# A spatial product of seven block products in place of eight, in a fused Fourier mixing and gated MLP kernel

## The chip, the cores and the metric

The kernel runs on one core of one Trainium2 chip. The metric is the device time of one execution in microseconds. Every kernel here was run several times, on a chip that also ran the kernel before; medians and ranges are given.

## The reference, cut to what matters

```python
X = np.fft.fft(np.fft.fft(x, axis=1), axis=2).real     # x: 8 batches, 3072 rows, 256 columns
h = np.maximum(X @ w_in, 0.0)                          # 1024 columns
u, v = h[..., :512], h[..., 512:]
v_n = (v - mean(v)) / np.sqrt(var(v) + 1e-06)          # row by row
v_s = np.einsum('ts,bsd->btd', w_spatial, v_n) + b_spatial[None, :, None]
out = (u * v_s) @ w_out
```

The heavy part is the spatial product: a 3072 x 3072 matrix times the 512 columns of v, for each of eight batches. The weights of that matrix are 0.01/3072 times a normal draw, and the bias beside it is 1. The output therefore hardly depends on the spatial product, and the comparison with the reference would not notice a mistake in it. For the experiments this means that a kernel with wrong block sums on purpose can still be called correct; where I did that, I say so.

Of the kernel before, what the change touches and what calls it, by code (L numbers as in the profile page):

```python
# [9 lines left out]
FP32 = mybir.dt.float32  # L10
# [23 lines left out]
NWR = 5  # L34
AHEAD = 4
# [13 lines left out]
VFIRST = [0, 1, 2, 4, 5, 7]  # L49
# [6 lines left out]
FOLD = [(2, 4), (8, 16), (18, 20)]  # L56
DCT = [36, 38, 40, 42]
VAT = [44 + (17 * i) // 4 for i in range(NPAIR)]
FOLD1 = [(12, 16), (24, 28), (36, 38)]
DCT1 = [40, 42, 44, 46]  # L60
VAT1 = [49 + (15 * i) // 4 for i in range(NPAIR)]
# [11 lines left out]
def kernel(  # L73
# [17 lines left out]
    wrpool = ctx.enter_context(tc.tile_pool(name="wrpool", bufs=NWR))  # L91
    wbpool = ctx.enter_context(tc.tile_pool(name="wbpool", bufs=3))
# [3 lines left out]
    upool = ctx.enter_context(tc.tile_pool(name="upool", bufs=8))  # L96
    gpool = ctx.enter_context(tc.tile_pool(name="gpool", bufs=6))
# [17 lines left out]
    bbc = const.tile([P, S], FP32)  # L115
# [19 lines left out]
    def load_x(b, a, xr):  # L135
        xt = xpool.tile([P, 8, D], FP32, name="xt", tag="xt")
        base = x.offset + b * S * D
        nc.sync.dma_start(out=xt[:, 0:4, :],
                          in_=bass.AP(x.tensor, base + (1 + a) * D,
                                      [[3 * D, P], [768 * D, 4], [1, D]]))  # L140
        nc.sync.dma_start(out=xt[:, 4:8, :],
                          in_=xr.rearrange("j p (r d) -> p j r d", r=3)[:, :, 2 - a, :])
        return xt[:, 0:4, :], view(xt, 7 * D, [[-D, 4], [1, D]])
# [13 lines left out]

    def load_w():
# [5 lines left out]
        wr = wrpool.tile([P, HW], FP32, name="wr", tag="wr")  # L164
# [14 lines left out]
    def cast_w(first=False):  # L179

        i = wstate["cast"]
        if i >= len(pieces):
            return
        c, g, r = pieces[i]
        wr = wrq[i]
        wbs[i] = wbpool.tile([P, HW], BF16, name="wb", tag="wb")
        src = wr if g % 2 == 0 else view(wr, HW - 1, [[-1, HW]])
        if first:
            nc.scalar.copy(out=wbs[i], in_=src)  # L189
        else:  # L190
            nc.gpsimd.tensor_copy(out=wbs[i], in_=src)  # L191
        wstate["cast"] = i + 1
        load_w()
# [23 lines left out]
    siota = bbc[:, 0:LQ]  # L217
# [11 lines left out]
    xs = xpool.tile([4 * B, D], FP32, name="xs", tag="xs")  # L229
# [48 lines left out]
    sp4 = spool.tile([4 * B, 6, 4 * B], FP32, name="sp4", tag="sp4", bufs=1)  # L278
# [77 lines left out]
    def fold_even(plus, rev):  # L356

        sm = fpool.tile([P, 4, D], FP32, name="sm", tag="sm")
        nc.vector.tensor_tensor(out=sm, in0=plus, in1=rev, op=ALU.add)
        e = ef  # L360
        nc.vector.tensor_copy(out=view(e, 0, [[129, 4], [128, 2]]),
                              in_=view(sm, 0, [[D, 4], [128, 2]]))
        nc.vector.tensor_tensor(out=e[:, :, 1:128], in0=sm[:, :, 1:128],
                                in1=view(sm, 255, [[D, 4], [-1, 127]]), op=ALU.add)
        evf = fpool.tile([P, 2, 129], FP32, name="evf", tag="evf")
        od = gxpool.tile([P, 2, 129], BF16, name="od", tag="od")
        ev = gxpool.tile([P, 2, 129], BF16, name="ev", tag="ev")
        nc.vector.tensor_tensor(out=od, in0=e[:, 0:2], in1=e[:, 2:4], op=ALU.subtract)
        nc.vector.tensor_tensor(out=evf, in0=e[:, 0:2], in1=e[:, 2:4], op=ALU.add)
        nc.vector.tensor_tensor(out=ev[:, 0], in0=evf[:, 0], in1=evf[:, 1], op=ALU.add)  # L370
        nc.vector.tensor_tensor(out=ev[:, 1], in0=evf[:, 0], in1=evf[:, 1],
                                op=ALU.subtract)
        return od, ev

    def fold_odd(plus, rev, od):


        df = plus
        nc.vector.tensor_tensor(out=df, in0=df, in1=rev, op=ALU.subtract)
        o = of  # L380
        nc.vector.tensor_tensor(out=o[:, :, 1:128], in0=df[:, :, 1:128],
                                in1=view(df, 255, [[df.ap[1][0], 4], [-1, 127]]),
                                op=ALU.subtract)
        ovf = fpool.tile([P, 2, P], FP32, name="ovf", tag="ovf")
        ho = gxpool.tile([P, 2, P], BF16, name="ho", tag="ho")
        he = gxpool.tile([P, 2, P], BF16, name="he", tag="he")
        nc.vector.tensor_tensor(out=ho, in0=view(o, 0, [[3 * P, 2], [1, P]]),
                                in1=view(o, 2 * P, [[-P, 2], [1, P]]), op=ALU.subtract)
        nc.vector.tensor_tensor(out=ovf, in0=o[:, 0:2], in1=o[:, 2:4], op=ALU.add)
        nc.vector.tensor_tensor(out=he[:, 0], in0=ovf[:, 0], in1=ovf[:, 1], op=ALU.add)  # L390
        nc.vector.tensor_tensor(out=he[:, 1], in0=ovf[:, 0], in1=ovf[:, 1], op=ALU.subtract)
        nc.vector.tensor_copy(out=view(ho, 0, [[P, 2], [1, 1]]),
                              in_=view(od, 129 + 128, [[-129, 2], [1, 1]]))
        return ho, he

    def specials():

        nb = 4 * B
        xe = gxpool.tile([nb, 129], BF16, name="xe", tag="xe", bufs=1)
        xo = gxpool.tile([nb, P], BF16, name="xo", tag="xo", bufs=1)  # L400
# [22 lines left out]
        sc = gxpool.tile([nb, 2, nb], BF16, name="sc", tag="sc", bufs=1)  # L423
# [17 lines left out]
    def specials_copy(pb):  # L441
        nc.vector.tensor_copy(out=spb, in_=pb[:, 0:2, :])
        nc.vector.tensor_copy(out=spb[0:1, 1, :], in_=pb[0:1, 2, :])

# [41 lines left out]
    def dct_odd(b, c, gx, eo):  # L486
# [17 lines left out]
        if b == 0 and c % 2 == 0:  # L504
            nc.scalar.activation(out=view(eo, EOW + c, [[4, n]]), in_=po_[:, 0:n],
                                 func=AF.Identity, bias=spb[:, 1, c:c + 1])
            return
        nc.vector.tensor_scalar(out=view(eo, EOW + c, [[4, n]]), in0=po_[:, 0:n],
                                scalar1=spb[:, 1, 4 * b + c:4 * b + c + 1],
                                scalar2=(sgn[:, 0:1] if c == 1 else None),  # L510
                                op0=ALU.add, **({"op1": ALU.mult} if c == 1 else {}))


    def v_rows(i, eo, pr, first):
# [3 lines left out]
        rs = spool.tile([P, 3], FP32, name="rs", tag="rs")  # L518
# [63 lines left out]
    def v_norm(i, v, pr):  # L582
        r, stt, mv, rs = pr.pop(i)
        k = 2 * GK * (i // GK) + i % GK
        nc.vector.reciprocal(out=rs[:, 0:2], in_=rs[:, 0:2])
        nc.vector.tensor_scalar(out=rs[:, 2:3], in0=mv[:, 0, 0:1], scalar1=rs[:, 0:1],  # L586
# [8 lines left out]
    def u_pair(c, dt, eo):  # L595
# [5 lines left out]
        for kt in range(2):  # L601
# [8 lines left out]
        nc.vector.tensor_tensor(out=view(um, TC - 1, [[-1, TC]]), in0=ps, in1=m_,  # L610
                                op=ALU.subtract)
        if c == 0:
            p1 = psM.tile([P, TC], FP32, name="pu1", tag="psM")
            for kt in range(2):
                nc.tensor.matmul(p1[:, 0:1], lhsT=weo[:, kt, wd],
                                 rhs=eo[:, kt, S // 2:S // 2 + 1], start=(kt == 0),
                                 stop=(kt == 1))
            nc.vector.tensor_copy(out=um[:, TC - 1:TC], in_=p1[:, 0:1])
# [8 lines left out]
    def gate(c, pw, ut):  # L627
        gt = gpool.tile([P, TC], BF16, name="gt", tag="gt")
        tm = tpool.tile([P, TC], FP32, name="tm", tag="tm")
        nc.vector.tensor_tensor(out=tm, in0=pw, in1=bbc[:, TC * c:TC * c + TC], op=ALU.add)  # L630
        nc.vector.scalar_tensor_tensor(out=gt, in0=ut, scalar=0.0, in1=tm, op0=ALU.max,  # L631
                                       op1=ALU.mult)
        return gt
# [32 lines left out]
    class Prep:  # L666
# [6 lines left out]
        def even(self, a):  # L673
            self.xt = xt0[a] if self.b == 0 else xin.pop((self.b, a))
            self.od, self.ev = fold_even(*self.xt)
            if self.b == 0:
                dct_part(a, (self.od, self.ev, None, None), self.pe0)

        def odd(self, a):
            ho, he = fold_odd(*self.xt, self.od)  # L680
            self.gx.append((self.od, self.ev, ho, he))
            if self.b > 0:
                if a + 1 < NA:
                    x_step(self.b, a + 1)
                else:
                    x_step(self.b + 1, 0)
# [9 lines left out]
        def v_steps(self, i):  # L696

            def va():
                if i == 0:
# [4 lines left out]
                    lambda: v_root(i, self.pr), lambda: v_norm(i, self.v, self.pr)]  # L704

        def v_first(self, i):
# [7 lines left out]
            if i > 0:  # L714
                v_norm(i - 1, self.v, self.pr)
# [3 lines left out]
        def steps(self):  # L719
# [3 lines left out]
            fold, dct, vat = (FOLD1, DCT1, VAT1) if self.b == 1 else (FOLD, DCT, VAT)  # L723
            if self.b == 1:
                st_[5].append(lambda: x_step(1, 0))
            for a in range(NA):
                s0, s1 = fold[a]
                st_[s0].append(lambda a=a: self.even(a))
                st_[s1].append(lambda a=a: self.odd(a))
# [3 lines left out]
            for i in range(NPAIR):  # L733
                for n, f in enumerate(self.v_steps(i)):
                    st_[vat[i] + n].append(f)
            return st_

    def load_wt(c, g):
# [140 lines left out]
```

## The kernel before: the parts that the change and the argument touch

Weights of the spatial product are turned and stored in HBM once, at the start. Later a batch streams them back as tiles of 768 KB (6 KB in a row for each of 128 partitions) into a ring of five buffers. Per batch there are six chunks of 512 output rows, and each adds up 24 products in each of four banks:

```python
def spatial(v, wt, pw, g, dt):
    for kk in range(GK):                       # GK = 6
        k = GK * g + kk
        nc.tensor.matmul(pw, lhsT=v[:, k, 128 * dt:128 * dt + 128], rhs=wt[:, kk, :],
                         start=(k == 0), stop=(k == KT - 1))

def gate(c, pw, ut):                           # two Vector operations
    ...
    nc.vector.tensor_tensor(out=tm, in0=pw, in1=bbc[:, TC * c:TC * c + TC], op=ALU.add)
    nc.vector.scalar_tensor_tensor(out=gt, in0=ut, scalar=0.0, in1=tm, op0=ALU.max,
                                   op1=ALU.mult)
```

Beside the spatial product of one batch, the next batch is prepared: x comes in thirds, Vector folds each third (sums and differences of mirrored rows), TensorE transforms the result, and v is formed and normalised. There is one buffer for a third of x, so the load of the next third can start only when the folds of the one before have finished. The load has two parts of 0.5 MB, and in the kernel before it stands in the same queue as the weight tiles, that of the Sync engine:

```python
def load_x(b, a, xr):
    xt = xpool.tile([P, 8, D], FP32, name="xt", tag="xt")       # xpool: one buffer
    ...
    nc.sync.dma_start(out=xt[:, 0:4, :], in_=...)
    nc.sync.dma_start(out=xt[:, 4:8, :], in_=xr...)

def load_wt(c, g):
    wt = wtpool.tile([P, GK, TC], BF16, name="wt", tag="wt")
    nc.sync.dma_start(out=wt, in_=wtd[c][g])
    return wt
```

## Time and profile before

| | kernel before | where it is read |
|---|---|---|
| time, median (range) | 1387.42 us (1385.82 to 1389.2) | four runs beside the changed kernel |
| span of the profiled run | 1384.1 us | head of the page |
| spatial matmuls | 4608, 0.216 us from start to start | groups and timeline of TensorE |
| one batch in the steady part | 158.4 us | first projections of two batches |
| Vector, Scalar in it | 101.5 us, 56.6 us | window |
| DMA in it | 160 GB/s, share 0.47 | window |

The prediction shows the lines for these. Three more follow. The first is from part 4 of the page, the chain of work that ended last: shares of the span by engine, followed backwards from the last instruction. The second fence is the timeline of the Sync engine, where a line stands for a DMA that it issued: start, time for the issue, queue, source line, destination<-source.

```profile
PE 87%; DMA 5%; DVE 3%; ACT 2%; POOL 2%; issue 1%; ACTq 0%; SPq 0%; POOLq 0%; DVEq 0%
```

```profile
629.34 0.50 SPq L141 DMA_DIRECT2D xt<-xr  x1
630.09 0.33 SPq L740 DMA_DIRECT2D wt<-wtd  x1
```

The chain is TensorE for 87% of the span. The other two lines show a third of x taking its turn in the order of the weight tiles: the next tile is issued after it.

### The profile page before, as it was taken

To read this page: it belongs to the slowest core of one execution; us is meant where nothing else is said; L and a number is where in the kernel's file an instruction comes from. 1 tells how busy PE (TensorE), PEld (TensorE's weight loads), DVE (VectorE), ACT (ScalarE), POOL (GpSimd) and SP (SyncE) were. 2 spreads that over 40 slices of the span, in tenths; PEclk is the share of its full clock that TensorE was granted. 3 is DMA by queue.
4 is the path that set the end of the run, shared out by engine and by line. 5 is a ranking of instruction groups with operands and counts; after the bars stand their busy time and mean duration, and the time that the engine had idled before them with its cause. 6 is when DMAs were issued, how large, how long until landed. Compare 5 with 4: busy or idle time off the path is not lost.

```text
span 1384.1 us, 18120 instructions
## 1 busy us (share of the span) xinstructions
PE 1321.3 (95%) x6967; PEld 651.3 (47%) x6967; DVE 842.1 (61%) x1694; ACT 516.9 (37%) x890; POOL 128.6 (9%) x167
## 2 busy tenths in 40 slices
PE   1768999999999999999999999999999999999998
PEld 0434455544444444444444444444444444444444
DVE  7656657775567747675557746776466746762323
ACT  7863146521444134531444224530445214441110
POOL 8355134410000000000000000000000000000000
PEclk9989999999999999999999999999999999999999
DMA  7899699785444543356344653456344553444441
GB/s 241 290 361 336 201 296 301 277 313 176 156 134 150 197 171 130 137 185 226 107 137 150 201 168 130 132 182 227 107 139 148 178 185 111 136 154 160 150 147 54
DMA packets 105254, 255.28 MB, mean 184 GB/s; under 512 B 17584, under 2 KB 64336, under 8 KB 105168
## 3 DMA queue, kind: packets, MB, share of 16 engines
q1 hardware_dynamic: 65840, 196.66, 42.3%
q10 hardware_dynamic: 29824, 44.05, 8.8%
q0 software_dynamic: 9504, 13.42, 3.1%
q8 instruction: 54, 0.88, 0.3%
q14 instruction: 32, 0.26, 0.1%
HBM read 210.80 MB, written 56.62 MB: 193 GB/s over the span
## 4 chain that ended last, share of the span: by engine, by line
PE 87%; DMA 5%; DVE 3%; ACT 2%; POOL 2%; issue 1%; ACTq 0%; SPq 0%; POOLq 0%; DVEq 0%
PE pw L624 68%; PE po L640 6%; DMA wr<-in_moe_w_spatial_dram 3%; PE pu L602 3%; PE pv L526 2%; PE pe L461 1%; PE pud L604 1%; PE pd L553 1%; PE pt L204 1%; DVE tm L630 1%; DMA xr<-in_x_dram 1%; DVE gt L631 1%; DMA wtd<-wx 1%; POOL xr L129 1%; POOL wb L191 0%
## 5 line engine op out<-in xcount | busy, mean ns | idle before, releaser
L624 PE MATMUL pw<-wt,v_t 128*128 128x512 bf16 x4512 | 1025.2, 380 | 7.8 <-ACT v_t L588 6.3
L624 PEld LDWEIGHTS <-v_t 128*128 128x128 bf16 x4608 | 446.4, 98 | 528.0 <-issue 10.8
L644 ACT COPY ot<-po 128x512 f32<-128x512 f32 x96 | 56.3, 586 | 403.6 <-PE po L640 392.2
L630 DVE TENSOR_TENSOR tm<-pw,bbc 128x512 f32<-128x512 f32 x192 | 131.5, 685 | 100.4 <-PE pw L624 90.3
L588 ACT ACTIVATE v_t<-r,rs 128x512 bf16<-128x512 f32 x96 | 78.4, 817 | 89.0 <-DVE rs L586 82.7
L640 PE MATMUL po<-wob,gt 128*128 128x256 bf16 x768 | 99.7, 273 | 1.7 <-DVE gt L631 1.7
L607 ACT ACTIVATE up<-pu 128x512 bf16<-128x512 f32 x96 | 57.3, 597 | 113.0 <-PE pu L602 73.6
L191 POOL CAST wb<-wr 128x768 bf16<-128x768 f32 x87 | 77.2, 893 | 134.8 <-PE pt L204 91.3
L640 PEld LDWEIGHTS <-gt 128*128 128x128 bf16 x768 | 74.7, 98 | 29.8 <-DVE gt L631 2.2
L574 DVE BATCH_NORM_STATS2 stt<-r 128x6 f32<-128x512 f32 x108 | 72.5, 680 | 23.6 <-ACT r L567 22.0
L204 PE MATMUL pt<-ident,wb 128*128 128x128 bf16 x576 | 48.9, 228 | 29.8 <-POOL ident L275 21.7
L580 ACT ACTIVATE rs<-mv,epst 128x2 f32<-128x2 f32 x96 | 28.5, 297 | 124.3 <-DVE mv L576 115.0
L631 DVE SCALAR_TENSOR_TENSOR gt<-up,tm 128x512 bf16<-128x512 bf16 x96 | 69.2, 720 | 3.3
L631 DVE SCALAR_TENSOR_TENSOR gt<-um,tm 128x512 bf16<-128x512 bf16 x96 | 67.2, 700 | 3.3
L204 PEld LDWEIGHTS <-wb 128*128 128x128 bf16 x576 | 41.0, 102 | 50.4 <-ACT wb L189 24.4
L567 ACT ACTIVATE r<-r 128x512 f32<-128x512 f32 x84 | 52.8, 628 | 28.2 <-DVE r L561 26.5
L526 PE MATMUL pv<-weo,eo_t 128*128 128x512 bf16 x192 | 57.8, 382 | 3.4 <-ACT r L536 2.7
L554 ACT ACTIVATE r<-pv 128x512 f32<-128x512 f32 x84 | 49.3, 587 | 27.0 <-PE pv L526 26.7
L602 PE MATMUL pu<-eo_t,weo 128*128 128x512 bf16 x192 | 57.5, 381 | 0.0
L562 DVE BATCH_NORM_STATS2 stt<-r 128x6 f32<-128x512 f32 x84 | 57.4, 684 | 0.0
L590 DVE TENSOR_SCALAR v_t<-r,mv,rs 128x512 bf16<-128x512 f32 x96 | 52.4, 546 | 0.0
L209 ACT COPY wt<-pt 128x768 bf16<-128x768 bf16 x44 | 35.1, 797 | 33.4 <-PE pt L204 33.3
(599 smaller groups left out, 1008.3 us busy)
## 6 DMA issues: line engine op xcount, KB each, us to landing
wt<-wtd SPq DMA_DIRECT2D x168, 768.0 KB, 4.4
wr<-in_moe_w_spatial_dram SPq DMA_DIRECT2D x69, 384.0 KB, 3.7
out_dram<-ot ACTq DMA_DIRECT2D x88, 256.0 KB, 3.9
wtd<-wt ACTq DMA_DIRECT2D x20, 768.0 KB, 5.3
xr<-in_x_dram POOLq DMA_DIRECT2D x32, 384.0 KB, 13.6
xt<-in_x_dram SPq DMA_DIRECT2D x21, 512.0 KB, 4.0
xt<-xr SPq DMA_DIRECT2D x21, 512.0 KB, 5.0
wr<-in_moe_w_spatial_dram SPq DMA_DIRECT2D x23, 383.5 KB, 7.0
```

Of the source, the lines that this page charges most:

```text
L191: nc.gpsimd.tensor_copy(out=wbs[i], in_=src)
L204: nc.tensor.transpose(pt[:, kk, :], wb[:, 128 * kk:128 * kk + 128], ident)
L526: nc.tensor.matmul(pv, lhsT=eo[:, kt, sl], rhs=weo[:, kt, DH:], start=(kt == 0), stop=(kt == 1))
L562: nc.vector.bn_stats(out=stt[:, 0, :], in_=r[0])
L574: nc.vector.bn_stats(out=stt[:, n, :], in_=r[n])
L588: nc.scalar.activation(out=v[:, k, :], in_=r[0], func=AF.Identity, scale=rs[:, 0:1], bias=rs[:, 2:3])
L602: nc.tensor.matmul(ps, lhsT=weo[:, kt, wd], rhs=eo[:, kt, sl], start=(kt == 0), stop=(kt == 1))
L607: nc.scalar.activation(out=up, in_=ps, func=AF.Relu)
L624: nc.tensor.matmul(pw, lhsT=v[:, k, 128 * dt:128 * dt + 128], rhs=wt[:, kk, :], start=(k == 0), stop=(k == KT - 1))
L630: nc.vector.tensor_tensor(out=tm, in0=pw, in1=bbc[:, TC * c:TC * c + TC], op=ALU.add)
L631: nc.vector.scalar_tensor_tensor(out=gt, in0=ut, scalar=0.0, in1=tm, op0=ALU.max, op1=ALU.mult)
L640: nc.tensor.matmul(po[:, i, :], lhsT=gts[dt][:, t0:t0 + 128], rhs=wob[:, dt, :], start=(dt == 0), stop=(dt == NDT - 1))
```

## The change

The intent is a Strassen-like product: a product of 2 x 2 blocks with seven block products in place of eight, at the price of sums of blocks. It is applied to batches 2 to 7. The sums of weight blocks (24 tiles) are made once, by Vector beside batch 1, and stored in HBM. The sums of v blocks are made for each batch by Vector in bf16: eight instructions of 1536 elements a partition, six of them at the start of the batch. Finished products are added into accumulators by Vector. To make room, the second half of the normalisation and the odd half of the transform move from Vector to Scalar (from the preparation of batch 3 on; half of the odd transform of batch 0 too), the positions of all steps were set anew, and the bias is loaded for each chunk. The loads of x for batches 2 to 7 go to Scalar's queue. The diff, cut to its core:

```diff
+        q = nc.scalar if b > 1 else nc.sync
-        nc.sync.dma_start(out=xt[:, 0:4, :], ...)
-        nc.sync.dma_start(out=xt[:, 4:8, :], ...)
+        q.dma_start(out=xt[:, 0:4, :], ...)
+        q.dma_start(out=xt[:, 4:8, :], ...)
...
-    def fold_even(plus, rev): ...
-    def fold_odd(plus, rev, od): ...
+    def fold_steps(plus, rev, res): ...          # the same work as six steps s0 to s5
...
+        if b > 2 or (b == 0 and c % 2 == 0):     # odd transform: Scalar in place of Vector
+            nc.scalar.activation(out=o_, in_=po_[:, 0:n], func=AF.Identity, scale=sg, bias=off)
...
+    def t_sum(v, k, h):                          # block sums of v
+        ...
+        nc.vector.tensor_tensor(out=o, in0=x_, in1=y_,
+                                op=ALU.add if k == 2 else ALU.subtract)
...
+    def after(p, d, pw, bt, bb, us):             # what a finished block product is added to
+        a0, a1, a2 = (acc(k, d) for k in range(3))
+        if p == 1:
+            plus(a1, pw, bb)
+            plus(a2, pw, bt)
+        elif p == 6:
+            plus(a1, pw, a1)
+            plus(a0, pw, a2)
+        elif p == 7:
+            plus(a1, pw, a1)
+        elif p == 4:
+            gate(a1, pw, us[d][1])
+        elif p == 2:
+            gate(a2, pw, us[d][0])
+        elif p == 5:
+            tm = gate_sum(a1, pw)
+            plus(a0, pw, a0)
+            gate_mul(tm, us[2 + d][1])
+        else:
+            gate(a0, pw, us[2 + d][0])
...
+ORDP = [1, 6, 7, 4, 2, 5, 3]                     # seven products, three chunks of 28 positions
+FOLD2 = [(0, 2, 3, 4, 5, 6), (12, 12, 13, 14, 17, 18), (25, 26, 27, 28, 28, 29)]
+DCT2 = [31, 32, 34, 35]
+TBEG = {0: (3, 1), 1: (2, 1), 4: (4, 0), 5: (4, 1), 8: (1, 1), 9: (1, 0)}
```

## The prediction

> **What bounds the kernel now.** I read the page first: how busy each engine is, then the slices.
>
> ```profile
> PE 1321.3 (95%) x6967; PEld 651.3 (47%) x6967; DVE 842.1 (61%) x1694; ACT 516.9 (37%) x890; POOL 128.6 (9%) x167
> ...
> PE   1768999999999999999999999999999999999998
> ```
>
> TensorE is full from about the fifth slice to the end; Vector has nearly two fifths of the span free. A busy PE row alone is not proof, since the matmuls overlap, so I looked at the costliest groups and at the order of time.
>
> ```profile
> L624 PE MATMUL pw<-wt,v_t 128*128 128x512 bf16 x4512 | 1025.2, 380 | 7.8 <-ACT v_t L588 6.3
> ...
> L630 DVE TENSOR_TENSOR tm<-pw,bbc 128x512 f32<-128x512 f32 x192 | 131.5, 685 | 100.4 <-PE pw L624 90.3
> ```
>
> The spatial product waited only 7.8 us in the whole run, while the evacuation behind it (L630) waited 90 us for TensorE: the consumer is idle, not the producer. The timeline of TensorE gives the real rate and the period of a batch:
>
> ```profile
> 287.80 1.04 PE L640 MATMUL po<-wob,gt 128*128 128x256 bf16 x8
> ...
> 446.22 1.04 PE L640 MATMUL po<-wob,gt 128*128 128x256 bf16 x8
> ...
> 1359.74 5.34 PE L624 MATMUL pw<-wt,v_t 128*128 128x512 bf16 x24
> 1364.92 1.04 PE L640 MATMUL po<-wob,gt 128*128 128x256 bf16 x8
> ```
>
> 24 spatial matmuls take 1364.92 - 1359.74 = 5.18 us from start to start, 0.216 us each, not the 380 ns of the group. The same first projection of batches 1 and 2 stands at 287.80 and 446.22: a batch is 158.4 us. Adding up one batch: 576 spatial matmuls 124.3; 96 projections of 256 columns at half the cost 10.4; 36 for u and 36 for v 15.5; 42 for the transform with 384 columns, 6.8; a few small ones, about 1. That is 158, so a batch is TensorE from end to end. The window of one such period, with the best-fed window of the start for comparison of transfers:
>
> ```profile
> core 0: us, PE busy (x) PEld busy (x) DVE busy (x) ACT busy (x) POOL busy (x), PEclk, DMA share, GB/s
> 478.57:636.99 158.42, 158.42 (x797) 76.56 (x796) 101.47 (x208) 56.61 (x101) 0.00 (x0) 1.00 0.47 160
> ...
> 60.00:105.00 45.00, 30.58 (x203) 16.00 (x202) 29.01 (x87) 30.68 (x58) 23.62 (x29) 0.89 1.01 364
> ```
>
> Columns that matter: in a steady batch Vector 101.5 us (64%), Scalar 56.6, DMA share 0.47 at 160 GB/s, granted clock 1.00. When the DMA engines were full they moved 364 GB/s. Batch 1 starts near 282.6 (287.80 less one tile of 5.18), batch 7 near 1233.4; the span is 1384.1, the timed median 1387.2, so 3 us more.
>
> [...]
> - [...] So a removed matmul is worth 0.216 us.
> - [...] The trace has 685 (L630) and 1217 to 1230 (the folds). [...] The trace has no such bf16 sum[...].
> [...]
>
> **The change, part by part.** TensorE: for batches 2 to 7 the 8 block products become 7, so 576 spatial matmuls a batch become 3 x 7 x 2 x 2 x 6 = 504. 72 x 0.2158 = 15.54 us a batch, 93.2 us in six. Everything else on TensorE stays. All of it lies on the path, since TensorE is the path. A full batch then is 158.42 - 15.54 = 142.9 us.
>
> Vector, one steady batch, by durations of this trace. Before, all instructions sum to about 107 us: 24 evacuations and 24 gates 33, normalisation 40, folds 21, u 9, odd transform 4.4. The window shows 101.5, because neighbours overlap a little: a factor of 0.95, which I apply to the new sum too. After: every finished block product must be added[...], into several outputs: 10 additions for each of 6 (chunk, half) pairs, 60 x 0.685 = 41.1, and 24 gates x 0.692 = 16.6: 57.7 in place of 33. [...] The second half of normalisation (12 x 0.537) and the odd transform (4.4) move to Scalar from the preparation of batch 3 on: v is left with 33.5. Folds 21, u 9. Sum 129, times 0.95 = 122 us in 142.9, 86%. Scalar: 56.6 + 12 x 0.817 + 4 x 1.12 = 71 us, half full, plus the issue of x loads.
>
> Batch 1 keeps its eight products (158.4 us of TensorE) but makes the block sums of the weights beside them: 3 chunks x 4 sums x 2 halves x 2 parts = 48[...], with two sums of v: [...]147 of 158, 93%.
>
> Transfers: 24 weight tiles of 0.786 MB a batch become 42, 33.0 MB; with x (3.1), its turned copy (1.6), output (3.1) and the bias rows now loaded per chunk (1.6) that is 42.4 MB in 142.9 us, 297 GB/s, against 160. By share, 0.47 x 297/160 = 0.87. Batch 1 stores 24 summed tiles: 47 MB in 158 us, 298 GB/s too.
>
> The sum with nothing lost: 1387.2 - 93.2 = 1294. It is the floor unless the start gets shorter; the bias broadcast leaves the crowded start, but that is worth a few us at most.
>
> **Where it may lose.** Averages hide the first third of a batch, where the folds and the first block sums of v are packed. By the step lists, positions 0 to 27: Vector has 19.2 of products, 17.5 of folds[...], 3.0 of u: 45.4 x 0.95 = 43 us. TensorE there has 168 x 0.2158 + 32 x 0.109 + 12 x 0.2158 = 42.4. So Vector is level with TensorE for that third and lags at each fold. A product's two banks are wanted again only after the next product, some 6 us, so I expect lags of 3 to 5 us to be mostly absorbed. The same third also wants 14 weight tiles (11.0 MB), the turned x, two x loads, outputs and bias: 16.3 MB in 42.6 us, 382 GB/s, above the 364 seen. The ring holds four tiles ahead (13 us of work), so it drains somewhat and refills later. More doubtful is the fold of the second third of x: it can be loaded only when Vector has finished the first (one buffer). Before, this wait was
>
> ```profile
> 634.36 1.23 DVE L359 TENSOR_TENSOR sm<-xt 128x1024 f32<-128x1024 f32 x1 [4.08 <-DMA xt<-xr]
> ```
>
> 4.08 us with half-empty DMA engines. With fuller ones Vector[...] may stand there with finished products behind it. I allow 2 to 3 us a batch for all of this in batches 2 to 6 (13 us), 1 in batch 7, whose Vector has no preparation to do, and 5 us in batch 1 for sums that wait for stores. Start: 0, give or take 3. 1294 + 13 + 1 + 5 = 1313; the step positions look placed by hand or search for just these lags, so I shade it to 1309.
>
> **Rivals.**
> - Nothing lost: TensorE stays the bound, 1294. For it: 86% and 93% are below 100, and positions are tuned. Against it: a full first third.
> - Vector becomes the bound. If each steady batch loses 6 to 8 us at the folds and batch 1 loses 15, the time is about 1340 to 1350. For it: the 43 against 42.4. Against it: 20 us of slack in the rest of the batch.
> - Block sums run at single rate[...]. Batch 1 then needs (107 + 50 x 1.76) x 0.95 = 185 us of Vector, 27 more than TensorE, and each batch 6 us more: about 1345 to 1355. No trace line excludes it[...].
> - DMA becomes the bound. If only 300 GB/s are reached (the first 20 us of the run had 301 at a share of 0.97), the first third would take 54 us, 12 more, in all six batches: about 1364. Against it: weight tiles are large (6 KB runs a partition), and the 364 were reached with smaller mixed pieces.
>
> None of them eats the whole 93 us, so slower is very unlikely; two together could come near the 2% mark (1359). Range 1296 to 1338. Chances: faster by over 2% 0.95, within 2% 0.04, slower 0.01.
>
> **What would show it.** Right: 4176 spatial matmuls still about 0.216 us from start to start; first projections of batches 3 and 4 some 143 to 147 us apart; PE busy about 98% of a steady window; Vector about 122 us of it;[...] batch 1 near 163 us; DMA share 0.85 to 0.9. Waits of spatial matmuls on Vector's additions would be a few us a batch, in its first third. Wrong: batch periods of 150 us and more, TensorE waiting mainly for wt transfers (DMA) or for Vector throughout, block sums of 1.7 us, or a start of batch 1 well after 283 us.

## The result, and the profile after

| | before | after |
|---|---|---|
| time, median (range), 4 runs each | 1387.42 (1385.82 to 1389.2) | 1328.43 (1327.63 to 1331.1) |
| span of the profiled run | 1384.1 | 1327.0 |
| mean granted clock | 0.995 | 0.98 |

The ratio is 0.9578 (95% interval 0.956 to 0.9596): the changed kernel is 4.2% faster. A ratio here is the mean time of one kernel's runs over that of the other's of the same rounds, so it is not quite the ratio of the medians quoted. The result is inside the predicted range and 19 us above the predicted 1309. Measured against the 1294 at which nothing would be lost, 34 us of the 93 expected are missing.

The page of the changed kernel, its slices and its chain:

```profile
PE 1234.6 (93%) x6411; PEld 611.7 (46%) x6535; DVE 986.8 (74%) x1927; ACT 566.9 (43%) x970; POOL 126.0 (9%) x167
...
PE   1777999998999999999899989999899989999998
...
PE 63%; DVE 18%; DMA 10%; ACT 3%; issue 3%; POOL 1%; ACTq 0%; SPq 0%; DVEq 0%; POOLq 0%
```

The row of TensorE, which had nines to the end before, now has an 8 every fourth or fifth slice from its middle on. A slice is 33 us, so the dips come once a batch. Vector has gone from 3% to 18% of the chain, DMA from 5% to 10%. The list of waits of TensorE (engine, line and what it waited for; us in total, times, longest) names the dip:

```profile
PE pe L509 <- DVE ev L413: 19.6, 4, 6.2
```

The even transform (pe) waited four times for ev, a product of Vector's folds, 19.6 us in all. The kernel before has no such line. Now one batch in windows; the first projection of batch 3 is at 590.29 and that of batch 4 at 740.54. The columns are named in the first line.

```profile
core 0: us, PE busy (x) PEld busy (x) DVE busy (x) ACT busy (x) POOL busy (x), PEclk, DMA share, GB/s
590.29:633.25 42.96, 42.40 (x216) 20.80 (x220) 38.28 (x73) 9.30 (x17) 0.00 (x0) 1.00 0.92 332
633.25:693.72 60.47, 55.66 (x270) 26.41 (x274) 39.69 (x80) 29.79 (x48) 0.00 (x0) 0.97 0.68 236
...
590.29:740.54 150.25, 144.34 (x713) 69.76 (x726) 116.43 (x235) 66.54 (x117) 0.00 (x0) 0.99 0.79 274
640.00:646.00 6.00, 3.38 (x10) 1.06 (x11) 5.86 (x13) 0.36 (x1) 0.00 (x0) 0.74 0.33 116
622.00:637.00 15.00, 14.95 (x75) 7.31 (x75) 7.85 (x18) 1.66 (x3) 0.00 (x0) 1.00 0.97 357
```

The batch took 150.25 us where 142.9 had been worked out. The first third, which the prediction feared, is busy with 42.40 of 42.96 us. The loss is at the start of the second third, around 640, where TensorE works 3.38 of 6 us at a clock of 0.74. Just before, from 622 to 637, the DMA engines are full (share 0.97) and Vector works only half of the time. The timelines of TensorE, Vector and Scalar there (in brackets the idle time before and what ended it):

```profile
642.62 0.34 PE L509 MATMUL pe<-ct,ev 128*128 128x385 bf16 x1 [4.54 <-DVE ev L413]
642.80 2.64 PE L1090 MATMUL pw<-wt,zone 128*128 128x512 bf16 x6
```

```profile
636.87 1.23 DVE L398 TENSOR_TENSOR sm<-xt 128x1024 f32<-128x1024 f32 x1 [6.84 <-DMA bt<-in_moe_b_spatial_dram]
```

```profile
621.92 0.52 ACTq L168 DMA_DIRECT2D xt<-xr  x1
```

Read upwards: Scalar issued the second half of the last third of x at 621.92, on its own queue. Vector stood 6.84 us until its first fold of that third began at 636.87, 15 us after the issue. It then had finished products to serve as well, so ev was ready only at 642.6, and TensorE had stood for 4.54 us. The page puts Vector's wait down to a bias row (bt), the transfer that landed last; in batches 4 and 5 the same wait, 8.47 and 6.49 us, is put down to xt itself. The view of the issuing line gives the time from issue to landing of those loads that the trace could follow, here two, both of a last third (the middle number is their mean):

```profile
DMA to landing us min/median/max: 14.9/15.7/16.6
```

In all four batches 3 to 6 Vector waited for the last third, and its fold began 14.6 to 16.6 us after the issue. The second third, on the same queue, was folded without a wait in each of them, in batch 3 some 7.8 us after its issue: few weights passed beside it (0.82 MB on the weights' queue against 1.50 MB on Scalar's in 605.2 to 612.8). Below, last thirds are compared with last thirds.

After the stop TensorE also ran slowly: six spatial matmuls from 642.80 took 2.64 us, where six take 1.46 at a clock of 1.00 (L624 of the kernel before, in its steady batch). After the gap of 4.54 us the mean clock was 0.74 in 640 to 646, and after those of 6.24, 4.20 and 4.57 us in batches 4 to 6 it was 0.51 in 795 to 800, 0.50 in 945 to 950 and 0.57 in 1096 to 1101.

The periods of batches 2 to 6 are 147.84, 150.25, 152.49, 150.32 and 150.44 us, together 36.9 us more than five times 142.9. The rest of the account, with a batch counted from its first weight load of the spatial product: batch 1 took 164.2 us in place of 158.4 (5.8 more), the last batch 136.9 to the end where 135.4 was left by the removed products (1.4 more), and batch 1 began at 274.7 in place of 282.4, so the start was 7.7 us shorter. 36.9 + 5.8 + 1.4 - 7.7 = 36.4 us above 1294 is 1330.4, within 2 us of the measured 1328.43.

### The profile page after: what moved, and what is told of

Read it like the earlier page. It is cut to its first block, busy times and chain, and to the rows that moved or that the text cites.

```text
span 1327.0 us, 17817 instructions
## 1 busy us (share of the span) xinstructions
PE 1234.6 (93%) x6411; PEld 611.7 (46%) x6535; DVE 986.8 (74%) x1927; ACT 566.9 (43%) x970; POOL 126.0 (9%) x167
## 4 chain that ended last, share of the span: by engine, by line
PE 63%; DVE 18%; DMA 10%; ACT 3%; issue 3%; POOL 1%; ACTq 0%; SPq 0%; DVEq 0%; POOLq 0%
PE pw L1090 33%; PE pw L681 13%; DMA xt<-xr 5%; PE po L714 4%; DMA zone<-in_moe_w_spatial_dram 3%; DVE tm L697 3%; PE pv L573 2%; PE pu L656 2%; PE pt L239 2%; DVE zone L947 2%; PE pe L509 1%; DVE um L701 1%; DVE up L701 1%; DMA bt<-in_moe_b_spatial_dram 1%; PE pd L600 1%
## 5 line engine op out<-in xcount | busy, mean ns | idle before, releaser
L1090 PE MATMUL pw<-wt,v_t 128*128 128x512 bf16 x1695 | 388.7, 380 | 3.4 <-DVE tm L697 1.4
L1090 PE MATMUL pw<-wt,zone 128*128 128x512 bf16 x1257 | 302.0, 384 | 3.2 <-DVE zone L934 1.2
L1090 PEld LDWEIGHTS <-v_t 128*128 128x128 bf16 x1728 | 168.9, 98 | 202.3 <-issue 5.0
L1090 PEld LDWEIGHTS <-zone 128*128 128x128 bf16 x1296 | 126.5, 99 | 144.9 <-issue 4.9
L681 PE MATMUL pw<-wt,v_t 128*128 128x512 bf16 x744 | 178.4, 379 | 5.0 <-ACT v_t L642 2.5
L681 PEld LDWEIGHTS <-v_t 128*128 128x128 bf16 x1152 | 111.3, 98 | 134.4 <-issue 9.4
L947 DVE TENSOR_TENSOR zone<-pw,zone 128x512 f32<-128x512 f32 x144 | 94.6, 681 | 71.1 <-PE pw L1090 70.8
L697 DVE TENSOR_TENSOR tm<-pw,zone 128x512 f32<-128x512 f32 x144 | 98.1, 682 | 34.1 <-PE pw L1090 30.3
L226 POOL CAST zone<-zone 128x768 bf16<-128x768 f32 x87 | 74.6, 860 | 129.0 <-PE pt L239 85.4
L701 DVE SCALAR_TENSOR_TENSOR up<-up,tm 128x512 bf16<-128x512 bf16 x96 | 69.5, 724 | 3.3
L681 PE MATMUL pw<-zone,v_t 128*128 128x512 bf16 x281 | 66.0, 386 | 3.7 <-DVE tm L697 3.3
L701 DVE SCALAR_TENSOR_TENSOR um<-um,tm 128x512 bf16<-128x512 bf16 x96 | 66.9, 697 | 2.1
L239 PEld LDWEIGHTS <-zone 128*128 128x128 bf16 x576 | 41.4, 103 | 52.6 <-ACT zone L224 25.2
```

Source lines behind the costliest of these rows:

```text
L226: nc.gpsimd.tensor_copy(out=wbs[i], in_=src)
L239: nc.tensor.transpose(pt[:, kk, :], wb[:, 128 * kk:128 * kk + 128], ident)
L697: nc.vector.tensor_tensor(out=tm, in0=pw, in1=a, op=ALU.add)
L701: nc.vector.scalar_tensor_tensor(out=ut, in0=ut, scalar=0.0, in1=tm, op0=ALU.max, op1=ALU.mult)
L947: nc.vector.tensor_tensor(out=o, in0=pw, in1=a, op=ALU.add)
L1090: nc.tensor.matmul(pws[d], lhsT=station(p, cur.v, h, j, d), rhs=wt[:, j, :], start=(h == 0 and j == 0), stop=(h == 1 and j == GK - 1))
```

## The experiments

Theory: the load of the last third of x lands too late. Three things might make it late, and the first four kernels were to tell them apart: the weight tiles that fill the engines, Vector's lag in its first third (which frees x late), and the place of the load in the order of steps.

### e_dma_light: fewer weight tiles around the load (failed)

```diff
 n = len(fetched)
+if n >= 42 and n % 42 in range(14, 22):
+    fetched.append(view(ct, 0, [[TC, GK], [1, TC]]))    # no load, wrong numbers on purpose
+    return
```

> Wrong result on purpose: from batch 3 on, eight weight tiles (the first eight of the second third) are not loaded; TensorE multiplies a constant table instead, so its work is unchanged, and the DMA engines are relieved by 6.3 MB just while the third x load of a batch is under way. Theory A (full DMA engines make that x load land after some 15 us, Vector waits for it, the transform's matmuls wait for Vector 4.2 to 6.2 us, and the granted clock then falls for a few us): the load lands in 9 us or less, the waits of the transform for ev vanish in batches 3 to 6, their periods fall from 150 to 152 us to 143 to 144, time about 1300. Theory B (Vector has too much work in the first third, whatever the DMA does): nothing moves, 1325 to 1330.

Measured: 1327.98 us (1322.56 to 1329.86), ratio 0.9566; wrong (relative error 30). The waits for ev are still there, 19.9 us in four. The experiment did not do what it was meant to. The ring fetched the tiles after the missing ones in the time that was freed, so the engines were as full as before:

```profile
630.00:635.00 5.00, 5.00 (x29) 2.65 (x27) 0.32 (x1) 1.45 (x3) 0.00 (x0) 1.00 1.03 408
```

It decides nothing. To relieve the engines, each tile must become smaller, not some tiles vanish; e_dma_half does that.

### e_vec_light: Vector without four of its six block sums in batches 3 to 7

```diff
 for t, (k, h) in TBEG.items():
+    if b > 2 and k in (1, 4):
+        continue                                        # wrong on purpose
     steps[t].append(...)
```

> Wrong result on purpose: from batch 3 on, four of the six block sums of v at the start of a batch (4 x 0.95 = 3.8 us of Vector) are left out; loads and TensorE unchanged. Theory B (Vector's work in the first third is the cause): the stall shrinks by about 3.8 us a batch, more with the clock, time about 1305 to 1312. Theory A in its strict form (only the transfer counts): at most what an earlier issue of the x load gives; if Vector catches up the load is issued up to 3.8 us earlier but still lands late, 1315 to 1328. The issue time of the third x load and its landing tell how much each has.

Measured: 1317.77 us (1315.8 to 1321.51), ratio 0.9501, 10.7 us less than the changed kernel. Its output is wrong, which doesn't matter for the time. The four waits for ev add up to 13.4 us, not 19.6. So Vector's load has a part. How it acts isn't shown: the last third of x was issued 30.3 to 31.2 us after a batch's first projection, hardly sooner than the 31.6 of the changed kernel in batch 3, and folded 13.2 to 17.4 us after its issue. It isn't the whole cause, since two thirds of the waits stay while 3.8 us of work a batch are gone.

### e_x_early: x freed earlier by another order of the folds

```diff
-self.fs[n]()
+self.fs[(0, 3, 4, 1, 2, 5)[n] if self.b > 2 else n]()   # the steps that read x come first
...
-if n == 5: ... x_step(...)
+if n == (2 if self.b > 2 else 5): ... x_step(...)       # and the next load follows at once
```

> Right result, same work: in the folds for batches 3 to 7 the three steps that read x come first, and the next x load is issued right after them, some three positions (4 to 6 us) sooner. Theory A: the loads land before Vector wants them or nearly so, the transform's wait goes from 4.2-6.2 us to 0-2 us in batches 3 to 6, and the clock stays up: 1300 to 1308. Theory B: the same Vector work in the same third, no gain: 1325 to 1330.

Measured: 1300.64 us (1299.7 to 1302.48), ratio 0.9377, correct. No wait for ev is left, and a batch takes 143.65 us. The last third of batch 3 was issued at 616.89, 26.9 us after that batch's first projection at 589.95; in the changed kernel it was 31.6 us (621.92 less 590.29). The engines are no less full, by the window of the same 15 us:

```profile
622.00:637.00 15.00, 15.00 (x78) 7.42 (x77) 14.55 (x28) 0.78 (x2) 0.00 (x0) 1.00 1.00 357
```

```profile
DMA to landing us min/median/max: 6.7/9.0/9.8
```

The same bytes pass, Vector is busy 14.55 of 15 us in place of 7.85, and 27.8 us are won. So the late load was the cause of most of the loss, and the number of bytes was not a limit. The landing numbers are of four loads; the last thirds among them took 9.8 and 6.7 us.

### e_dct_late: the transform and normalisation three positions later

```diff
-DCT2 = [31, 32, 34, 35]
+DCT2 = [34, 35, 37, 38]
-VAT2 = [37, 39, 43, 47, 52, 56, 59, 61, 65, 68, 72, 76]
+VAT2 = [40, 42, 46, 49, 53, 57, 60, 63, 66, 69, 73, 77]
```

> Right result, same work: only the positions of the transform (three later) and of the normalisation pairs (one to three later) are moved in batches 3 and later, so TensorE comes to the transform some 4 to 5 us later. Theory A and B alike: the wait of the transform for ev falls by about that, to 0-2 us, and the lowered clock behind it with it, 1300 to 1310, unless the later pairs squeeze Vector in the last third, where it has 38.5 of 46.8 us. If the lost time is not this wait but TensorE's slower clock or Vector's evacuations generally, it stays at 1325 to 1330.

Measured: 1317.89 us (1315.08 to 1320.17), ratio 0.9499. This missed what the theory expected. The waits for ev are mostly gone, but waits for Scalar come in their place, because the moved steps now meet others on that engine; in TensorE's timeline:

```profile
692.69 0.38 PE L600 MATMUL pd<-wo,eo_t 128*128 128x512 bf16 x1 [1.83 <-ACT m__7090 L663]
```

There is one such wait of 1.8 us in every batch, and others of 1 to 1.8 us. The load itself stayed late (the last third was folded 11.7 to 15.3 us after its issue); TensorE only came later to its result. A consumer can be moved away from a late producer, but only into a place that is free on every engine concerned.

### e_x_on_sp: the loads of x back on the queue of the weight tiles

```diff
-q = nc.scalar if b > 1 else nc.sync
+q = nc.sync
```

> Right result: only the queue of the x loads is put back to the one that it had before the change (the weight tiles' queue) for batches 2 and later. If the x load is slow because, in a queue of its own, its 1 KB pieces take turns with the 6 KB pieces of several weight tiles, it now waits only for the tiles ahead of it[...]: landing 8 us or less, stall gone, 1298 to 1310. If the total of bytes alone counts, it lands as late as before: 1322 to 1330. If its wait for Vector's fold holds up the weight tiles behind it by more than the ring's lead, TensorE waits for tiles: over 1330.

Measured: 1298.86 us (1296.72 to 1299.84), ratio 0.9362 (0.9348 to 0.9377), correct. This undoes one line of the change, and it is 29.6 us faster than the changed kernel, the best of all kernels here. Its windows (first third, the 54 us after it, the batch, and the same 15 us as above) and the landing of the same load:

```profile
588.03:630.30 42.27, 41.71 (x213) 20.41 (x217) 40.77 (x77) 8.74 (x17) 0.00 (x0) 1.00 0.86 313
631.10:685.20 54.10, 53.84 (x270) 26.20 (x274) 36.34 (x75) 30.09 (x48) 0.00 (x0) 1.00 0.79 278
588.03:731.67 143.64, 142.61 (x713) 69.48 (x726) 116.33 (x235) 66.84 (x117) 0.00 (x0) 1.00 0.81 286
622.00:637.00 15.00, 14.95 (x78) 7.48 (x78) 14.55 (x28) 2.24 (x4) 0.00 (x0) 1.00 0.96 360
```

```profile
DMA to landing us min/median/max: 4.9/5.5/7.6
```

The load was issued at 619.66, 31.6 us after the batch's first projection, just as late as in the changed kernel. The DMA engines moved 360 GB/s in those 15 us, just as many as there (357). But the load landed after some 5 us: the line is of eight loads, and the two last thirds among them took 5.3 and 4.9 us, where the changed kernel's took 14.9 and 16.6. The time of issue and the bytes are thus the same, and what differs is which queue the load stood in. My guess of why: alone on its queue, a load with rows of 1 KB gets a small part of the bytes while several tiles with rows of 6 KB pass beside it; on the weights' own queue it only stands in line. These landings agree with that but don't show it; e_tiles_in_thirds puts it to a test.

### e_dma_half: 16 of the 42 tiles loaded by half

```diff
+if n >= 42 and n % 42 in range(5, 21):
+    nc.sync.dma_start(out=wt[:, 0:3], in_=operand(*stream[n])[:, 0:3])   # wrong on purpose
```

> Wrong result on purpose, and the repair of e_dma_light, in which the queue simply fetched later tiles in the freed time, so that the DMA engines stayed as full as before: here the sixteen weight tiles fetched during the first third of batches 3 to 7 are loaded by half (and the half is multiplied twice), at the same pace and with the same waits. TensorE and Vector are unchanged; 6.3 MB a batch are taken from the transfers. Theory A (full DMA engines are why the third x load takes 15 us): it lands in 7 us or less, no wait of the transform for ev in batches 3 to 6, periods 143 to 145 us, time 1298 to 1306. Theory B (Vector's lag alone, which makes the load be issued late): landing may shorten but the stall stays above 3 us, 1318 to 1328.

Measured: 1300.90 us (1298.73 to 1304.25), ratio 0.9381. Its output is wrong, which doesn't matter for the time. The waits for ev are gone:

```profile
622.00:637.00 15.00, 14.89 (x73) 7.24 (x74) 14.57 (x28) 1.66 (x3) 0.00 (x0) 1.00 0.78 246
```

```profile
DMA to landing us min/median/max: 5.4/6.3/7.1
```

These are two last thirds. With the x loads still on their own queue, a lighter weight queue cures the stall as well. So it takes both, full engines and a queue apart. This edit also shortened the rows from 6 KB to 3 KB, so it does not separate fewer bytes from smaller packets.

### e_tiles_in_thirds: the same bytes in rows of 2 KB, x on its own queue

```diff
-nc.sync.dma_start(out=wt, in_=operand(*stream[len(fetched)]))
+src = operand(*stream[len(fetched)])
+for i in range(0, GK, 2):
+    nc.sync.dma_start(out=wt[:, i:i + 2], in_=src[:, i:i + 2])
```

> Right result: x stays on its own queue as in the changed kernel, and the same bytes are loaded; but each weight tile of batches 2 to 7 comes as three transfers with runs of 2 KB a partition in place of one with 6 KB. e_x_on_sp showed the x load landing in 5.5 us (median) at the same 360 GB/s, so the total of bytes is not what made it late. If the engines take turns between the two queues[...]: landing about 8 to 10 us in place of 15.7, the stall of the transform 0 to 1 us, 1298 to 1308. If the turns do not depend on the size of the pieces (what counts is only standing behind several tiles, or a fixed share of a queue), landing stays at 14 us or more and the time at 1322 to 1330.

Measured: 1323.82 us (1318.64 to 1327.81), ratio 0.9538. There is no wait for ev, and the landing line reads

```profile
DMA to landing us min/median/max: 7.9/8.5/9.8
```

This line is of three loads, all of second thirds. The last thirds were folded 8.0 to 9.8 us after their issue, in place of 14.6 to 16.6. In batch 3 that proves little: from 622 to 637 the engines moved only 275 GB/s here, since Sync issued no weight tile from 623.6 to 629.2. Its issues now waited for x loads to land, which they do not in the changed kernel (in the view of waits; SPq is Sync's sequencer):

```profile
SPq L1016 <- DMA xt<-in_x_dram: 37.6, 10, 5.7
```

Batch 4 is a fair test. Its last third was issued at 772.88 and folded at 780.92, without a wait, with the engines full; in the changed kernel it was issued at 772.24 and folded at 788.82, at 357 GB/s.

```profile
772.90:780.90 8.00, 8.00 (x39) 3.64 (x38) 7.69 (x17) 0.00 (x0) 0.00 (x0) 1.00 1.03 363
```

The view of the DMA queues shows what passed beside the load. q1 is Sync's queue, with the weight tiles, and q10 Scalar's, with x; behind each stand packets, MB and share of the 16 engines' time. First 777 to 787 in the changed kernel, then 777 to 780 here:

```profile
q1 hardware_dynamic: 798, 3.59, 93.2%
q10 hardware_dynamic: 280, 0.27, 7.9%
```

```profile
q1 hardware_dynamic: 496, 0.91, 84.7%
q10 hardware_dynamic: 229, 0.22, 21.4%
```

The last quarter of the load, some 0.25 MB in small packets, needs 10 us beside the large packets (4.5 KB on average, 3.59 MB in 798) and 3 us beside the small ones (1.8 KB, 0.91 MB in 496). So the load got 0.27 of 3.86 MB there and 0.22 of 1.13 MB here: in these runs its part of the bytes, and with it the landing, went with the packets beside it, as I had guessed. The time did not follow, though, because of a new stall that I had not foreseen. In Scalar's timeline:

```profile
647.29 0.24 ACTq L726 DMA_DIRECT2D out_dram<-ot  x1
647.58 1.11 ACT L511 ACTIVATE eo_t<-pe,spb 128x385 bf16<-128x385 f32 x1 [6.79 <-DMA out_dram<-ot]
```

Scalar stood 6.79 us around four issues of output stores and formed the transform's output eo_t late; TensorE then waited 8.5 us for it, in three waits, and the clock fell again, to 0.82 in 645 to 650 and 0.50 in 650 to 655. What held the issues isn't shown: the view names only a store. In the changed kernel the wait at the same place is 1.75 us. So I take this stall and Sync's waits above for side effects of the edit. The expectation holds for the load and fails for the time.

### e_x_early_late_projection: the wait at the start of batch 2

In the changed kernel as in its variants, TensorE waits 0.95 and 1.24 us at the start of batch 2 for Vector's last gates of batch 1. On top of e_x_early the first projection of batch 2 was put some positions later:

```diff
-if q in PROJ and PROJ[q][0] < len(pend):
-    project(*pend[PROJ[q][0]], PROJ[q][1])
+pj = {4: (0, 0), 5: (0, 1)} if (b, c) == (2, 0) else PROJ
+if q in pj and pj[q][0] < len(pend):
+    project(*pend[pj[q][0]], pj[q][1])
```

> Right result; e_x_early (1300.6) plus one edit: at the start of batch 2 the projection of batch 1's last chunk is made two to three positions later, since TensorE waited there 2.2 us (0.95 + 1.24) for Vector's last gates. If that wait is only a matter of position, it goes: about 1298. If Vector is so late there that the next product waits instead, 1300 as before.

Measured: 1300.84 us (1299.74 to 1301.37), ratio 0.9378, against 1300.64 for e_x_early: no gain. In place of the wait there is one of 2.84 us for v from Scalar.

### e_x_early_sp: both cures together

The edits of e_x_early and e_x_on_sp in one kernel.

> Right result; both cures at once: x loads on the weight tiles' queue, and issued earlier. Each alone gave 1298.9 and 1300.6, with hardly a wait left in batches 3 to 6, so nothing should add up: 1297 to 1301. A gain of more than 2 us would mean that each left a part of the stall.

Measured: 1307.95 us (1306.31 to 1309.36), ratio 0.9429. This is 7 to 9 us worse than either cure alone, and my expectation missed. TensorE waits 9.0 us in ten places for weight tiles. The timeline of the Sync engine shows why:

```profile
633.70 0.39 SPq L168 DMA_DIRECT2D xt<-xr  x1
634.17 0.46 SPq L1015 DMA_DIRECT2D wt<-std  x1
634.68 7.95 SPq L690 DMA_DIRECT2D bt<-in_moe_b_spatial_dram  x2
```

The two issues before these, weight tiles, end at 627.65; the next is the first half of the load of x at 633.15, just after Vector's last read of the buffer ends (633.12, L422), and the next weight tile comes only after the second half, at 634.17. The load stands earlier in the queue here, but Vector hadn't freed the buffer, and the weight tile behind it waited too. The issues of two bias rows that follow took 7.95 us.

### e_sums_on_pool and e_pool_x_on_sp: four of six block sums on GpSimd

The rival here was that Vector's first third is the limit, so its sums might go to the engine that stands idle. The edit, on the changed kernel and then on e_x_on_sp:

```diff
-nc.vector.tensor_tensor(out=o, in0=x_, in1=y_, ...)
+eng = nc.gpsimd if k in (1, 4) else nc.vector
+eng.tensor_tensor(out=o, in0=x_, in1=y_, ...)
```

> Right result: the four block sums of v that e_vec_light left out are made by the idle GpSimd instead of Vector, in all batches from 2 on. If GpSimd works beside Vector for nothing, Vector is relieved by 3.8 us as in e_vec_light: about 1318, or less as batch 2 gains too. If the two engines hinder each other at SBUF (Vector's two-input instructions grow longer while GpSimd sums), the gain is eaten: 1325 to 1345. [...]the product that uses it is some products away, so TensorE should not wait for it.

> Right result: e_sums_on_pool again, on the base of e_x_on_sp (1298.9), so that the late x load no longer mixes in. If GpSimd's four sums a batch (3.1 to 3.3 us each, seen in e_sums_on_pool) hinder Vector's two-input instructions in SBUF, as seen there (an 8-element copy of 2.18 us, a 508-element sum of 3.52 us in place of 0.69), Vector loses about 9 us a batch for the 3.8 saved, in the third in which it has no slack: some 5 us of stall a batch, 1320 to 1345. If the loss of e_sums_on_pool was all the x load: 1296 to 1300.

Measured: 1360.37 us (1358.41 to 1362.47), ratio 0.9808, and 1356.85 us (1354.85 to 1357.48), ratio 0.977. Both are above the upper ends that I had given (1345), and both are worse than their base kernels (e_sums_on_pool against the kernel before is unclear at 2%). A sum took 3.1 to 3.3 us on GpSimd against 0.95 on Vector. Vector meanwhile became slower, by its timeline in e_sums_on_pool and, for the same two operations, in the changed kernel:

```profile
608.34 2.18 DVE L402 COPY ef<-sm 128x8 f32<-128x8 f32 x1
610.55 3.52 DVE L404 TENSOR_TENSOR ef<-sm 128x508 f32<-128x508 f32 x1
613.99 1.28 DVE L947 TENSOR_TENSOR zone<-pw,bt 128x512 f32<-128x512 f32 x2
```

```profile
598.73 0.17 DVE L402 COPY ef<-sm 128x8 f32<-128x8 f32 x1
598.93 0.69 DVE L404 TENSOR_TENSOR ef<-sm 128x508 f32<-128x508 f32 x1
```

A small copy grew from 0.17 to 2.18 us and a sum of two SBUF operands from 0.69 to 3.52. Two additions with a PSUM operand take 1.28 us in both kernels. GpSimd was at three sums from 607.39 to 617.02, and the slow operations of Vector lie in that time; by which mechanism the two engines hinder each other isn't shown. A second cost comes on top: GpSimd also issues the turned copies of x. In e_pool_x_on_sp a set of four was issued only at 618.30, behind the sums, of which the last two took 6.58 us from 611.77; in the changed kernel GpSimd has nothing to do in that batch. Vector stood 22.3 us for loads of x in e_pool_x_on_sp, in six waits. How much of the loss belongs to each of the two isn't separated.

### e_double_sums_x_on_sp: how much room Vector has in the first third

On e_x_on_sp, four of the six early block sums of each batch are made twice.

```diff
-steps[t].append(lambda k=k, h=h, v=cur.v: t_sum(v, k, h))
+for _ in range(2 if k != 1 else 1):
+    steps[t].append(lambda k=k, h=h, v=cur.v: t_sum(v, k, h))
```

> Right result (the repeated sums give the same again): on the base of e_x_on_sp, four of the six block sums at the start of each of batches 2 to 7 are made twice, 3.8 us more of Vector in the first third, where it is busy 40.8 of 42.3 us. If the first third is at Vector's limit and the lag can't be absorbed, each batch grows by 2 to 4 us: 1311 to 1323. If the banks and the free time in the second third absorb it: 1299 to 1303.

Measured: 1316.56 us (1315.7 to 1317.85), ratio 0.9484, correct. It is 17.7 us above e_x_on_sp, 2.95 us for each of six batches, for 3.8 us of Vector work more in each. In TensorE's timeline:

```profile
599.46 2.74 PE L1091 MATMUL pw<-wt,zone 128*128 128x512 bf16 x6 [2.28 <-DVE zone L934]
```

Most of an addition to Vector in the first third is an addition to the time, though over the whole batch Vector is busy only 116 of 144 us. In e_x_on_sp it is busy 40.77 of 42.27 us there: no loss yet, and no room.

## Why the prediction was right or wrong

**The bound and the removed work: right.** The count of TensorE's weight loads for the spatial product fell from 4608 to 4176, as worked out, and a removed matmul was worth its 0.216 us: once the new stall is undone (e_x_on_sp), a batch takes 143.6 us against 142.9 predicted, and the whole is 4.9 us above the floor of 1294. Batch 2 is 2.5 us longer there than worked out (145.4), batches 3 to 6 are 0.7 to 1.8 us longer. The 4.9 is not all of what is lost, since batch 1 also begins 6.0 us sooner there than in the kernel before.

**The engines' load: right in kind, somewhat too high.** Vector was busy 116.4 us a steady batch (122 predicted), Scalar 66.5 (71). No line of the kernel before shows what a block sum in bf16 takes; its part in the totals for Vector (122 us, 147 in batch 1, 43 in a first third) was my estimate. It took 0.94 to 0.95 us, so the rival with sums of 1.76 us falls. (That long Vector took in the kernel before for an operation of 1540 fp32 elements, L313.) The transfers ran at 274 GB/s (297 predicted) in the batch and 332 in its first third (382 predicted). The turned copy, 1.6 MB, was counted in every batch; all of those copies were in fact issued by 284 us. Without it the first third has 14.7 MB in 43 us, 342, near the measured 332. The DMA rival falls too.

**Batch 1: right. The start: shorter than allowed.** Batch 1 took 164.2 us; I had 163 (158.4 and 5 for sums that wait for stores). It began 7.7 us sooner than before, where I had put 0, give or take 3. I had named the bias broadcast, which leaves the start, as worth a few us; whether it is that or the new positions was not tested.

**The first third: right that it is level, and that the lag itself is absorbed.** I had 43 us of Vector against 42.4 of TensorE; the trace has 38.3 in the changed kernel and 40.8 in e_x_on_sp, in 43.0 and 42.3 us. There is no great stall of TensorE inside it. The doubled sums show that it is full.

**The step that failed** is the one about the fold of "the second third of x", with its allowance "2 to 3 us a batch for all of this in batches 2 to 6 (13 us)". The mechanism was right: Vector stands before a load of x with finished products behind it. But it was the last third, not the second (that was used without a wait in batches 3 to 6), and the term was 36.9 us, 4.9 to 9.6 a batch. The line that I showed for it, at 634.36, was already the fold of the last third, and my "half-empty DMA engines" was a mean over a longer stretch: in the 5 us before that fold their share was 0.84. The allowance was too small for two reasons. I had taken "fuller engines" as what makes the load slower, and priced the move to Scalar's queue as Scalar's issue time only. The full engines alone cost almost nothing: at 360 GB/s the last third on the weights' queue lands in some 5 us. The queue of its own, in which a transfer of small rows runs beside large ones, cost the last third 10 us of landing (14.9 and 16.6 us in place of 5.3 and 4.9) at the same issue time and the same rate of bytes; undoing it gave back 29.6 us. And I counted no second effect: behind each of the four stalls, of 4.20 to 6.24 us, TensorE's mean clock was 0.50 to 0.74 for 5 or 6 us.

Of the allowances, 13 for these folds stood against 36.9; 5 for batch 1 and 1 for batch 7 held (5.8 and 1.4); the 4 us shaded off for well-placed steps were not borne out; and the start gave 7.7 us that were not counted. That the start hid about a third of what the folds were off by is luck. The range held since its upper end lay 44 us above the floor.

**What stays open.** How the DMA engines divide their time between two queues isn't shown. The landings of the last third (14.6 to 16.6 us, 8.0 to 9.8 and some 5) and the packets of the two queues (280 and 798, 229 and 496) show only the outcome, and the views don't say which engine moved a packet. Landings on Scalar's queue also vary with the moment: 9.8 and 6.7 us for two last thirds in e_x_early at the same rate of bytes. What the remaining 0.7 to 1.8 us a batch in e_x_on_sp consists of isn't settled, nor why the start is shorter.

## What to carry to other kernels

When an edit moves a transfer to another queue, price the landing beside what fills the engines, not only the issue: a load with small rows, alone on a queue beside a stream of large ones, waited three times as long here with the same bytes moving (14.9 and 16.6 us against 5.3 and 4.9, at 357 and 360 GB/s). Look for the stretch in which the engines are level, not at averages over a stage: with 116 of 144 us busy, Vector had no room where it mattered, and neither "idle" GpSimd nor two cures together brought the sum of what each had promised. An experiment that undoes one line of a large change can be worth more than a new idea; the best kernel here is the change without its move of the x loads, 1298.86 us, 6.4% under the kernel before.
